# A fused attention and SwiGLU kernel: the last two blocks' down projection by two levels of seven products

## The chip, the cores and the metric

The kernel runs on one core of a Trainium2 chip. Time is device time in microseconds (us), the median of several runs. Engines: TensorE (PE, with its weight loads PEld), VectorE (DVE), ScalarE (ACT), GpSimd (POOL), SyncE (SP, which here only issues DMAs).

## The reference

All in fp32. Attention without softmax, then a feed-forward block on its output, seen as 4608 rows of 512:

```python
kv = np.einsum('bhsd,bhse->bhde', k, v)          # (8, 8, 576, 64) each
out = np.einsum('bhsd,bhde->bhse', q, kv)
rms = np.sqrt(np.mean(out * out, axis=-1, keepdims=True) + 1e-06)
x = (out / rms * g_norm) -> (4608, 512)
g = x @ w_gate                                   # 512 x 1536
silu = g * (1.0 / (1.0 + np.exp(-g)))
return (silu * (x @ w_val)) @ w_out              # 1536 x 512
```

## The kernel before, in words

The 4608 tokens are nine blocks of 512. A block's feed-forward part has an up stage (`x @ w_gate` and `x @ w_val`, silu, product: the hidden values `h`, stored with the hidden dimension on partitions) and a down stage (`h @ w_out`).

A matrix product is not done by eight block products but by seven, in the Winograd form of Strassen's scheme: sums of operand blocks are made first, and the seven products are added up in a chain. The products have the numbers 1 to 7; `CHAIN` (L629) says which of three PSUM tiles (`a`, `b`, `c`) each accumulates in. Class `Quad` (L640) holds one such scheme. `Up` does it for blocks 0 to 2. From block 3 (`PAIRED`) on, two blocks go up together (class `Pair`, L1219), by two levels: `Inner` (L757) does the seven inner products of a group of outer products (`GROUPS`, L765), for both blocks in one matmul of 256 columns; the weights' sums at both levels ("leaves") were made early, written to a scratch tensor `w` in HBM, and are streamed back by `Stream` (L879) into the nine tiles of `t_pool`. `pump` (L895) loads the next as soon as a tile comes free. In the up stage VectorE adds what comes from PSUM, ScalarE copies, and GpSimd makes some further sums: `made1` to `made3` (L837 to L864) add results of the groups, multiply by silu, and make the first-level sums of `h` that the down stage needs.

The down stage (class `Down`, L985) has one level: per block seven products over six hidden pairs with two token halves, 12 matmuls of 128x128 weights (here `h`) by 256 columns (of `w_out` or of its sums `t`, made by GpSimd in `turn_t`). Its rows come out with tokens on partitions and are stored in pieces of up to 512 KB (`Ffn.store`). For the last block (`final`) the last two products and sums are cut in halves, so that the last store is small. Two blocks of a pair go down one after the other (L1439 to L1444).

What sets the order: the whole is traced in Python, and a scheduler places instructions by engine with their semaphores; `in_order` (L135) keeps an engine's instructions as traced, and `tc.issue_after` puts one behind another. For pairs, TensorE's down stage stands as written. SP issues nearly all DMAs, in order; each DMA waits for the one before it on its semaphore, of which there are eight for SP and ACT together. Helpers `add`, `sub` and `mul` have lines 130 to 132, so these sums show under those lines, whoever asks for them.

Of the kernel before, what the change touches and what calls it, by code (L numbers as in the profile page):

```python
# [8 lines left out]
F32 = mybir.dt.float32  # L9
# [9 lines left out]
def kernel(  # L19
# [84 lines left out]
    kvs = [consts.tile([P, NS, D], F32, name=f"kv{i}") for i in range(3)]  # L104
# [29 lines left out]
    @contextmanager  # L134
    def in_order(*engines):  # L135

        traced = nc.cur_bb.bb.instructions
        last = traced[-1]
        yield
        start = next(k for k in reversed(range(len(traced))) if traced[k] is last) + 1  # L140
        before = {}
        for i in traced[start:]:
            if engines and i.engine not in engines:
                continue
            if i.engine in before:
                tc.add_manual_dep(
                    i, before[i.engine].name,
                    mybir.DependencyInfo(mybir.DependencyClass.NoSync, mybir.DependencyReason.DATA), reason="order",
                )
            before[i.engine] = i  # L150

# [488 lines left out]
    class Quad:  # L640


        def __init__(self, steps):
            self.steps = steps
            self.ps, self.room = {}, None

            self.apart = {}

# [3 lines left out]
        def multiply(self, p):  # L652
            name, first = CHAIN[p]
            if first:
                tiles = [PSUMS[name].tile([P, 2, HB], F32, name=name) for _ in range(1 + (name in self.apart))]
                self.ps[name], self.apart[name] = tiles[0], tiles[-1]
            banks = self.ps[name], self.apart[name]
            for e, i in self.order(p):
                lhsT, rhs = self.operands(p, e, i)

                self.ffn.multiplied = nc.tensor.matmul(  # L661
                    banks[e][:, e], lhsT=lhsT, rhs=rhs, start=first and i == 0 and (e == 0 or banks[0] is not banks[1]),
                    stop=i == self.steps - 1, skip_group_check=True,
                )
            getattr(self, f"after{p}", lambda: None)()
# [91 lines left out]
    class Inner:  # L757
# [94 lines left out]
        def made3(self, p, e, q):  # L852
            if p != 4:
                return
            h = h_both[:, :, 2 * self.j : 2 * self.j + 2]
            halves = lambda t: t.rearrange("p (b e) t -> p b e t", b=2)
            c11, c12, c21, c22 = (self.whole(*i) for i in ((1, 1), (3, 1), (3, 0), (1, 0)))

            engine = nc.gpsimd if self.j + 1 < NP else nc.vector
            mul(engine, h[:, :, :, 0:HB], halves(c11), halves(c12))  # L860
            with tc.issue_after(self.ffn.fifth.ins):
                nc.scalar.activation(out=c21, in_=c21, func=ACT.Silu)
            mul(engine, h[:, :, :, HB:BLK], halves(c21), halves(c22))
            self.ffn.ended = self.ffn.a.h_sums(self.j, 1, engine)  # L864

# [13 lines left out]
    class Stream:  # L879
# [15 lines left out]
        def pump(self):  # L895

            while self.next and not self.held[-9]:
                n, j, c = key = self.next.pop(0)
                tile_ = t_tile(key)
                os, ps = JOINT[c]  # L900
                count = len(os) * len(ps)
                self.tiles[key] = tile_.rearrange("p a (b c) -> p (a b) c", c=P)
                self.uses[key] = count
                to = self.tiles[key][:, 0:count].rearrange("p (o i) c -> p o (i c)", o=len(os))
                src = self.dram[:, j, steps_of(OUTERS, os), steps_of(INNERS, ps)].rearrange("p o i c -> p o (i c)")
                nc.sync.dma_start(out=to, in_=src)

        def use(self, n, j, o, p):
            c, i = self.joint[o, p]
            key = n, j, c  # L910
            self.uses[key] -= 1
            if not self.uses[key]:
                self.free(key)
            return self.tiles[key][:, i]
# [4 lines left out]
    stream = Stream()  # L919
# [65 lines left out]
    class Down(Quad):  # L985
        def __init__(self, ffn):
            super().__init__(NP)
            self.ffn = ffn
            self.t = {}
            self.final = ffn.n == NB - 1  # L990
            self.lone = False
            self.opens = None
            self.keeps = False
            if self.final:
                self.apart["c"] = None
# [16 lines left out]
        def multiply(self, p, es=(0, 1)):  # L1012
            if p == 3 and self.lone:
                self.third(es)
                return
# [7 lines left out]
        def third(self, es):  # L1023


            if es[0] == 0:
                tiles = [m_psum.tile([P, 2, HB], F32, name="m") for _ in range(1 + self.final)]
                self.thirds = tiles[0], tiles[-1]
            for e in es:
                for i in range(self.steps):  # L1030
                    lhsT, rhs = self.operands(3, e, i)
                    self.ffn.multiplied = nc.tensor.matmul(  # L1032
                        self.thirds[e][:, e], lhsT=lhsT, rhs=rhs, start=i == 0 and (e == 0 or self.final),
                        stop=i == self.steps - 1, skip_group_check=True,
                    )
            if not self.final:
                add(nc.vector, self.o1[:, :, HD:DM], self.thirds[0], self.u2)
                self.ffn.store(self.o1, 0)
                return
            for e in es:  # L1040
                add(nc.vector, self.o1[:, e, HD:DM], self.thirds[e][:, e], self.u2[:, e])
                self.ffn.store(self.o1[:, e : e + 1, HD:DM], e, slice(HD, DM))

        def after6(self):
            super().after6()
            if self.lone:
                self.add_c(self.u2, self.u2)

        def order(self, p):
            order = [(e, i) for e in range(2) for i in range(self.steps)]  # L1050
            return order if p == 3 and self.final else sorted(order, key=lambda ei: ei[1])
# [17 lines left out]
        def rows(self):  # L1069
            o = ring()  # L1070
            self.o1, self.o2 = o[:, 0:2], o[:, 2:4]

        def after2(self):
            if self.lone:
                self.rows()
            add(nc.vector, self.o1[:, :, 0:HD], self.ps["a"], self.s)
            if self.final:
                self.ffn.store(self.o1[:, :, 0:HD], 0, slice(0, HD))
# [4 lines left out]
        def after7(self):  # L1083
            if not self.lone:
                self.rows()
            u3 = self.piece(2)
            nc.scalar.copy(out=u3, in_=self.ps["b"])
            self.add_c(self.o2[:, :, HD:DM], u3)
# [5 lines left out]
        def after3(self):  # L1094
            self.add_c(self.o1[:, :, HD:DM], self.u2)
            if not self.final:
                self.ffn.store(self.o1, 0)
                return
            for e in range(2):
                self.ffn.store(self.o1[:, e : e + 1, HD:DM], e, slice(HD, DM))  # L1100

        def add_c(self, o, u):

            if not self.final:
                add(nc.vector, o, self.ps["c"], u)
                return
            for e, c in enumerate((self.ps["c"], self.apart["c"])):
                add(nc.vector, o[:, e], c[:, e], u[:, e])

    class Ffn:  # L1110
# [9 lines left out]
        def store(self, o, t, columns=slice(None)):  # L1120
            rows = out[BLK * self.n : BLK * (self.n + 1), columns].rearrange("(t p) d -> p t d", t=T)
# [40 lines left out]
        def down(self, nxt, then={}):  # L1162
# [3 lines left out]
            down.lone = nxt is None  # L1166
            order = (1, 6, 5, 7, 2, 4, 3) if 5 in fill else (1, 5, 6, 7, 2, 4, 3)
            if down.lone:
                order = (1, 5, 6, 2, 7, 3, 4)
            for p in order:  # L1170
# [5 lines left out]
                with tc.issue_after(nxt.multiplied.ins) if self.n == 0 and p in (5, 6) else ExitStack():  # L1176
                    down.multiply(p, *[(0,)] * (p == 3 and down.lone and down.final))
# [14 lines left out]
            if down.lone and down.final:  # L1192
                down.multiply(3, (1,))
# [25 lines left out]
    class Pair:  # L1219


        def __init__(self, n):
            self.n = n
            self.a, self.b = (Ffn(i, blocks[i]) for i in (n, n + 1))
            self.visited = None

        def up(self, fill):

            a = self.a
            a.s1 = s_pool.tile([P, NP, HB], F32, name="s1")  # L1230
# [5 lines left out]
            for i, this in enumerate(units):  # L1236
                for unit, p in this.sequence(last):
                    if unit:
                        visited, self.visited = self.visited, None
                        with tc.issue_after(visited.ins) if visited else ExitStack():  # L1240
                            unit.multiply(p)
                last = this
                fill.get(i + 1, lambda: None)()
            a.down_ = Down(a)
            a.down_.keeps = True
            a.down_.turn_t(5)
# [3 lines left out]
            a.ended = self.ended  # L1250
# [165 lines left out]
    for n in range(PAIRED, NB, 2):  # L1416
# [3 lines left out]
        if after:  # L1420
# [10 lines left out]
            for i in range(8):  # L1431
                fill[12 + i] = lambda i=i, after=after: after[i // 4].load_quarters(i % 4 // 2, (i % 2,))
        pair.up(fill)
        if after:
            after[0].turn()
        if len(after) > 2:
            after[2].load_kv(0)
        with in_order(nc.tensor.engine):
            pair.a.down(after[0] if after else None, {5: pair.second_sums})  # L1439
            if after:  # L1440
                after[1].turn()
            if len(after) > 2:
                after[2].load_kv(1)
            pair.b.down(after[1] if after else None)  # L1444
# [31 lines left out]
```

## Time and profile before

| | us |
|---|---|
| median of three runs (1011.41 to 1013.13) | 1011.48 |
| profiled execution | 1012.7 |
| its span, first to last instruction | 1010.9 |
| TensorE busy in the span | 993.7 |
| VectorE, GpSimd, ScalarE busy | 673.7, 369.6, 232.2 |
| last pair's down stage, TensorE | 934.85 to 1007.37 |

Busy time is the union of an engine's instructions. A row of the profile names line, engine, operation, written and read tile, shape and number; after the bar stand the busy us, the mean ns of one instruction, and the engine's idle time before it with what ended it. An fp32 matmul stands as two records, a transpose as one. The profile reports the granted clock of TensorE as 1.0 throughout.

### The profile page before, as it was taken

The numbers are of one execution on the slowest core, as the hardware profiler recorded it, in microseconds if no ns is written. First come the engines' busy times: TensorE is split into PE (matmuls) and PEld (weight loads), VectorE is DVE, ScalarE is ACT, GpSimd is POOL, SyncE is SP. The second block draws the span as 40 slices with busy tenths as digits, with TensorE's granted clock in tenths as the row PEclk, the third lists the DMA queues.
The fourth block names the chain that finished last, engine by engine and source line by source line (L and its number), as shares of the span: only waits on it lengthen the run. The fifth ranks groups of instructions, "written<-read, shape, count | busy, mean of one in ns | idle before, by whom it ended". The sixth has DMA issues, their size and how long they took to land.

```text
span 1010.9 us, 17078 instructions
## 1 busy us (share of the span) xinstructions
PE 993.7 (98%) x6506; PEld 831.6 (82%) x6506; DVE 673.7 (67%) x1121; ACT 232.2 (23%) x367; POOL 369.6 (37%) x290
## 2 busy tenths in 40 slices
PE   5999999999999999999999999999999999999998
PEld 4544688888888888888888888888888888888887
DVE  2999797589868477656676746666668566666311
ACT  2665111221122311212211121121112121121000
POOL 0000263255544240445456004455660026546600
PEclk9999999999999999999999999999999999999999
DMA  8688653483866855767742464667221654553011
GB/s 220 198 266 260 120 93 136 97 288 97 210 136 122 214 114 158 189 179 182 170 130 42 111 164 135 182 164 191 77 42 43 146 164 144 150 145 101 1 42 42
DMA packets 254290, 143.23 MB, mean 142 GB/s; under 512 B 149504, under 2 KB 236544, under 8 KB 254208
## 3 DMA queue, kind: packets, MB, share of 16 engines
q1 hardware_dynamic: 223488, 138.20, 50.8%
q10 hardware_dynamic: 30656, 3.94, 2.5%
q8 instruction: 52, 0.85, 0.4%
q14 instruction: 30, 0.25, 0.1%
q0 software_dynamic: 64, 0.00, 0.0%
HBM read 104.99 MB, written 28.70 MB: 132 GB/s over the span
## 4 chain that ended last, share of the span: by engine, by line
PE 75%; DMA 1%; POOL 0%; SPq 0%; issue 0%; DVE 0%; POOLq 0%
PE b L816 22%; PE b L661 20%; PE c L816 11%; PE c L661 9%; PE a L816 5%; PE a L661 5%; PE m L431 1%; PE m L1032 1%; PE m L370 1%; DMA ld<-in_v_dram 1%; POOL t L131 0%; SPq L312 0%; PE b L370 0%; PE b L431 0%; PE a L431 0%
## 5 line engine op out<-in xcount | busy, mean ns | idle before, releaser
L816 PE MATMUL b<-arena,t 128*128 128x256 f32 x1008 | 244.5, 381 | 0.0
L816 PEld LDWEIGHTS b<-arena,t 128*128 128x128 f32 x1008 | 190.1, 190 | 29.6 <-DVE r L130 2.4
L130 POOL TENSOR_TENSOR r<-r 128x256 f32<-128x256 f32 (+1 forms) x90 | 94.7, 1054 | 246.1 <-DVE r L130 154.9
L130 DVE TENSOR_TENSOR r<-b,r 128x512 f32<-128x512 f32 (+1 forms) x234 | 138.9, 606 | 60.1 <-PE b L816 54.8
L130 DVE TENSOR_TENSOR r<-c,r 128x512 f32<-128x512 f32 (+1 forms) x170 | 104.5, 623 | 81.9 <-PE c L816 40.1
L132 POOL TENSOR_TENSOR arena<-r 128x1024 f32<-128x1024 f32 (+1 forms) x54 | 102.1, 1904 | 112.3 <-DVE r L130 67.9
L131 POOL TENSOR_TENSOR t<-wo 128x512 f32<-128x512 f32 x54 | 76.9, 1445 | 167.8 <-DVE wo L130 105.9
L130 DVE TENSOR_TENSOR r<-a,r 128x512 f32<-128x512 f32 x93 | 59.2, 636 | 108.3 <-PE a L661 70.7
L816 PE MATMUL c<-arena,t 128*128 128x256 f32 x504 | 122.5, 379 | 0.0
L131 DVE TENSOR_TENSOR arena<-arena 128x512 f32<-128x512 f32 (+3 forms) x96 | 104.3, 1101 | 20.0 <-PE b L661 17.7
L816 PEld LDWEIGHTS c<-arena,t 128*128 128x128 f32 x504 | 95.6, 190 | 13.5 <-issue 0.3
L661 PE MATMUL b<-wo,arena 128*128 128x256 f32 x432 | 98.1, 382 | 0.2
L661 PE MATMUL b<-t,arena 128*128 128x256 f32 x432 | 96.2, 379 | 0.0
L661 PEld LDWEIGHTS b<-wo,arena 128*128 128x128 f32 x432 | 81.2, 190 | 12.5 <-DVE arena L132 0.9
L661 PEld LDWEIGHTS b<-t,arena 128*128 128x128 f32 x432 | 82.1, 190 | 11.2
L830 ACT COPY r<-b 128x512 f32<-128x512 f32 x54 | 31.7, 586 | 189.9 <-PE b L816 189.9
L131 POOL TENSOR_TENSOR t<-arena 128x512 f32<-128x512 f32 x36 | 51.1, 1432 | 56.2 <-PE c L661 21.9
L816 PE MATMUL a<-arena,t 128*128 128x256 f32 x252 | 66.1, 379 | 0.0
L816 PEld LDWEIGHTS a<-arena,t 128*128 128x128 f32 x252 | 47.9, 190 | 6.5
L661 PE MATMUL c<-t,s 128*128 128x256 f32 x216 | 48.1, 379 | 0.0
L661 PE MATMUL a<-wo,arena 128*128 128x256 f32 x216 | 48.1, 379 | 0.0
L661 PEld LDWEIGHTS a<-wo,arena 128*128 128x128 f32 x216 | 41.0, 190 | 5.6
(115 smaller groups left out, 1242.9 us busy)
## 6 DMA issues: line engine op xcount, KB each, us to landing
t<-w SPq DMA_DIRECT2D x180, 256.0 KB, 3.1
out_dram<-r SPq DMA_DIRECT2D x17, 512.0 KB, 2.9
ld<-in_k_dram SPq DMA_DIRECT2D x26, 288.0 KB, 4.6
ld<-in_v_dram SPq DMA_DIRECT2D x26, 288.0 KB, 6.1
t<-w SPq DMA_DIRECT2D x54, 128.0 KB, 2.3
ld<-in_moe_w_gate_dram SPq DMA_DIRECT2D x12, 512.0 KB, 4.6
ld<-in_moe_w_val_dram SPq DMA_DIRECT2D x12, 512.0 KB, 4.7
ld<-in_moe_w_out_dram SPq DMA_DIRECT2D x12, 512.0 KB, 4.8
```

The costliest lines, as they stand in the source:

```text
L130: add = lambda e, o, a, b: e.tensor_tensor(out=o, in0=a, in1=b, op=OP.add)
L131: sub = lambda e, o, a, b: e.tensor_tensor(out=o, in0=a, in1=b, op=OP.subtract)
L132: mul = lambda e, o, a, b: e.tensor_tensor(out=o, in0=a, in1=b, op=OP.mult)
L370: self.positions = nc.tensor.matmul(self.kv_ps[r][u * D : (u + 1) * D, g, :], lhsT=k[:, u, c, :], rhs=v[:, u, c, :], start=(c == 0), stop= ...
L431: self.multiplied = nc.tensor.matmul(self.ps[i][u][p : p + D, t, j, :], lhsT=self.qt[rows, tile_t, head, p : p + D], rhs=kvs[b % 3][rows, ...
L661: self.ffn.multiplied = nc.tensor.matmul(banks[e][:, e], lhsT=lhsT, rhs=rhs, start=first and i == 0 and (e == 0 or banks[0] is not banks[1 ...
L816: self.ffn.multiplied = nc.tensor.matmul(ps[:, i], lhsT=stream.use(self.ffn.n, self.j, o, p), rhs=self.operand(o, p), start=first and i == ...
L830: copied = nc.scalar.copy(out=dst, in_=ps)
L1032: self.ffn.multiplied = nc.tensor.matmul(self.thirds[e][:, e], lhsT=lhsT, rhs=rhs, start=i == 0 and (e == 0 or self.final), stop=i == self ...
```

## The change

Only the last two blocks (7 and 8) are treated differently; they go up as before. `Down` loses its special forms for the last block.

- Both blocks go down together, by two levels of seven products (`Last`, a kind of `Inner`, and `Deep`). Now the weights are the stationary operand and `h` of both blocks moves, 2 x 128 columns; results come out with the output dimension on partitions, in four groups of outer products (1, 2), (6, 5), (7), (4, 3).
- The second-level sums of `w_out` are made by GpSimd in the up stage of the pair, one side step after certain products (`tick`): the first-level sum in place, twelve sums kept in SBUF (`kept`), and for the outer products 5, 7 and 4 nine "turned blocks" of sums, which go to a scratch tensor `leaf` in HBM by SP (two stores, six products after their sums) and come back through the stream as 21 tiles.
- First-level sums of `h` are made in place by GpSimd 12 products after the values; second-level sums of `h` by VectorE in the down stage (`sum_x`, `outer`), which also does the last unit's (`second`, `turn`).
- In the end two quarters of the result are turned by VectorE in 32x32 blocks and stored by 16 DMAs each on ACT's and SP's queues (`send`); the other two by 16 PE transposes, copied by ScalarE and VectorE and stored by eight DMAs of SP (`turn_back`).
- The three `kv` tiles become one (a turned block's sums borrow one of them).

```diff
-    kvs = [consts.tile([P, NS, D], F32, name=f"kv{i}") for i in range(3)]
+    kv_room = consts.tile([P, 3, NS * D], F32, name="kv")
+    kvs = [kv_room[:, i].rearrange("p (j d) -> p j d", d=D) for i in range(3)]
...
+            if self.ffn.deep:
+                self.ffn.deep.made(self.j, engine, c21, halves(c21), halves(c22), h)
+                return
...
+    class Last(Inner):
+        GROUPS = ((1, 2), (6, 5), (7,), (4, 3))
...
+            for c in cs:
+                for i, o in enumerate(self.outers):
+                    self.ffn.multiplied = nc.tensor.matmul(
+                        ps[:, i], lhsT=self.deep.weight(o, p, c), rhs=self.deep.operand(o, p, c),
+                        start=first and c == 0 and i == 0, stop=c == 2, skip_group_check=True,
+                    )
+            stream.pump()
...
+            if p in self.ADDED:
+                add(nc.vector, dst, ps, dst)
+            elif self.g == 3:
+                add(nc.vector, dst, ps, self.shared[2][:, :, :, e, q])
+            elif self.g == 0:
+                nc.scalar.copy(out=dst, in_=ps)
+            else:
+                add(nc.vector, dst[:, 0], ps[:, 0], self.onto[:, :, e, q])
+                if n > 1:
+                    nc.scalar.copy(out=dst[:, 1], in_=ps[:, 1])
...
+        def turned_block(self, i, c):
...
+            def send():
+                with behind(nc.sync.engine):
+                    nc.sync.dma_start(out=to[:, 0:5], in_=t)
+                    nc.sync.dma_start(out=to[:, 5:7], in_=more)
+
+            def differences():
+                sub(nc.gpsimd, t[:, 4], t[:, 0], t[:, 1])
+                sub(nc.gpsimd, more, t[:, 2:4], t[:, 1:2].to_broadcast([P, 2, P]))
+                self.sends.append((self.count + 6, send))
...
+        FIRST = {0: (0, 1, 3), 1: (0, 2, 4), 2: (1, 4), 3: (0, 2, 4, 5)}
+        TURNS = {0: (0, 1), 1: (), 2: (4,), 3: (0, 2, 4, 5)}
+
+        def tick(self):
+            g, e = divmod(self.count % 28, 7)
+            self.count += 1
+            if self.sends and self.sends[0][0] <= self.count:
+                self.sends.pop(0)[1]()
+            due = self.due and self.due[0][0] <= self.count
+            if due and (g, e) in ((2, 5), (2, 6)):
+                step = self.due.pop(0)[1]
+            elif e in (self.TURNS if self.count > 28 else self.FIRST)[g]:
+                step = self.due.pop(0)[1] if due else self.later.pop(0) if self.later else None
...
+        def made(self, j, engine, c21, g, v, h):
...
+            steps = [lambda: add(engine, a21, a21, a22), lambda: sub(engine, a21, a21, a11)]
...
+            self.due += [(self.count + 12, step) for step in steps]
...
+        def send(self, room, half, cols, queue):
...
+                    for r in range(4):
+                        dst = out[row : row + HB, col + 32 * r : col + 32 * (r + 1)]
+                        queue.dma_start(
+                            out=dst.rearrange("(c i) j -> i c j", i=32), in_=t[32 * r : 32 * (r + 1), f, e]
+                        )
+
+        def turn_back(self, e, q, final=False):
+            ps = m_psum.tile([P, 2, 2, P], F32, name="m")
+            for o in range(2):
+                for f in range(2):
+                    nc.tensor.transpose(ps[:, o, f], self.shared[3][:, o, f, e, q], ident)
+            to = self.rows[:, e, q]
+            if final:
+                for o in range(2):
+                    nc.vector.tensor_copy(out=to[:, o], in_=ps[:, o])
+            else:
+                nc.scalar.copy(out=to, in_=ps)
...
+                nc.sync.dma_start(out=blocks_[row : row + P, :, col : col + P], in_=to[:, o])
+
+        def down(self):
...
+            run(self.turn(2, 0))
+            m(0, 1, (0, 1))
+            m(0, 2, (0, 1))
+            m(0, 1, (2,))
+            self.sum_x(0, 1, 2)
+            m(0, 2, (2,))
+            m(0, 6)
+            self.sum_x(1, 1, 2)
+            m(0, 5)
+            self.sum_x(2, 1, 2)
+            self.second()
+            run(self.turn(2, 1))
+            m(0, 7)
+            self.outer(5, ((0, 0), (0, 1)))
+            m(0, 3)
+            m(1, 1)
+            self.sum_x(0, 6, 5)
...
+            m(2, 4)
+            nc.vector.transpose(out=room[:, 0], in_=c11)
+            self.send(room[:, 0], 0, 0, nc.scalar)
+            m(3, 6)
+            add(nc.vector, c22, u3, c22)
+            m(3, 5)
+            nc.vector.transpose(out=room[:, 1], in_=c22)
+            self.send(room[:, 1], 1, 1, nc.sync)
+            m(3, 2)
+            m(3, 7)
+            self.rows = ring().rearrange("p (e q) (o f d) -> p e q o f d", e=2, o=2, f=2)
+            m(3, 3)
+            self.turn_back(0, 0)
+            self.turn_back(1, 1)
+            m(3, 4)
+            self.turn_back(1, 0)
+            self.turn_back(0, 1, True)
...
+        if pair.deep:
+            stream.leaves(pair.deep)
+            pair.up(fill)
+            with in_order(nc.tensor.engine, nc.vector.engine):
+                pair.deep.down()
+            continue
```

## The prediction

> **What bounds the kernel now.** I read first the page's busy shares and its chain that ended last, then the chain in order of time for the last 80 us, then the groups of instructions and the timeline there. The whole page:
>
> ```profile
> span 1010.9 us, 17078 instructions
> PE 993.7 (98%) x6506; PEld 831.6 (82%) x6506; DVE 673.7 (67%) x1121; ACT 232.2 (23%) x367; POOL 369.6 (37%) x290
> ```
>
> TensorE is the bound; the other engines have room on average. The chain at the end (start, length, engine, tile, line, matmul records), and the timeline behind it:
>
> ```profile
> 992.00 5.18 PE b L661 x24
> 997.18 2.59 PE m L1032 x12
> 999.77 5.18 PE b L661 x24
> 1004.95 2.60 PE m L1032 x12
> 1007.58 0.42 DVE L130 TENSOR_TENSOR r<-m,r 128x256 f32<-128x256 f32 x1 [7.35 <-PE m L1032]
> ```
>
> One fp32 product of 12 matmuls is 24 records and 5.18 us: 0.216 us a record, 0.432 a matmul. The last two blocks' down stage is 14 such products, starts at 934.85 and issues its last at 1007.37: 72.5 us with no gap. After it stand an eviction (0.42, done at 1008.00) and a store; the span ends 2.88 later. What this stage leaves to the others:
>
> ```profile
> 930.00:951.00 21.00, 21.00 (x98) 18.25 (x97) 9.73 (x13) 2.05 (x3) 14.04 (x10) 1.00 0.00 1
> 951.00:972.00 21.00, 21.00 (x99) 18.47 (x99) 4.43 (x5) 1.35 (x3) 4.61 (x4) 1.00 0.07 26
> 972.00:990.00 18.00, 18.00 (x85) 15.86 (x84) 2.51 (x3) 1.17 (x2) 0.00 (x0) 1.00 0.08 29
> ```
>
> Columns are length, then busy us of PE, PEld, DVE, ACT and POOL: VectorE and GpSimd are nearly idle where the change puts work. Prices, by shape:
>
> ```profile
> L494 PE MATMUL m<-ident,r 128*128 128x128 f32 x16 | 2.3, 274 | 0.3 <-DVE r L132 0.3
> L131 DVE TENSOR_TENSOR arena<-arena 128x896 f32<-128x896 f32 x3 | 3.3, 1089 | 0.1
> L132 DVE TENSOR_TENSOR arena<-r 128x1024 f32<-128x1024 f32 x2 | 2.4, 1222 | 0.1
> L130 DVE TENSOR_TENSOR s<-arena 128x256 f32<-128x256 f32 x1 | 0.4, 424 | 0.0
> L386 DVE STREAM_TRANSPOSE r<-ld 128x1024 f32<-128x1024 f32 x16 | 19.3, 1226 | 0.0
> L132 POOL TENSOR_TENSOR arena<-r 128x1024 f32<-128x1024 f32 x10 | 23.4, 2363 | 19.0 <-DVE r L130 19.0
> L131 POOL TENSOR_TENSOR t<-wo 128x512 f32<-128x512 f32 x4 | 5.1, 1274 | 4.5 <-DVE arena L131 4.5
> L130 POOL TENSOR_TENSOR r<-r 128x256 f32<-128x256 f32 x24 | 17.4, 727 | 71.0 <-DVE r L130 70.4
> ```
>
> A PE transpose has one record: 2.3/16 = 0.144 us. VectorE from SBUF: 0.42 at 256 elements, 1.09 at 896, so 0.96 at 768 and 0.69 at 512; an eviction is 0.69 (512) or 0.41 (256). GpSimd: 0.73 at 256, 1.27 at 512, so 1.00 at 384 and 0.46 at 128.
>
> **What the Trainium skill says.** "SBUF — State Buffer", Who interferes with whom: a VectorE instruction with two SBUF inputs and a GpSimd instruction that reads SBUF exclude each other for the whole instruction; one with at most one SBUF input doesn't. The trace agrees: at 356.59 a 1536-element difference took 2.42 beside GpSimd's sums instead of 1.75, while no eviction from PSUM in the last pair's up stage is longer than 0.69 beside GpSimd. "DMA: Bandwidth & Descriptors", Specifications: below 512 B a transfer costs a read-modify-write; no run here shows 128-byte writes to HBM. No page bears on the order of the products.
>
> **The change, part by part.** By the built order nothing before the last pair is moved, nor are its waits; all that follows is after 800 us.
>
> *TensorE.* 168 matmuls go, 147 of the same size come (49 products, 3 steps each): -21 x 0.432 = -9.07 us. 16 transposes come; 8 stand between the last two products, +1.15. The last matmul would issue at 934.87 + 63.46 + 1.15 = 999.5.
>
> *GpSimd, up stage.* From 803 on its list goes from 65 sums (34 of 256, 15 of 512, 16 of 1024: 82 us, the last at 955) to 103 (9 of 128, 33 of 256, 12 of 384, 33 of 512, 16 of 1024: 120 us, nearly all of it by 938). I walked its queue in the built order, unit by unit (21.15 us each): 17.5, 18.2, 19.3, 21.2, 19.3 us busy, before 11.4. In the fourth unit it is full, and the made-over sums behind a side sum start up to 2.6 us late, but their readers come some 5 us later: 0 us, as long as its rows hold. The six differences in place in the output weight start at 803.5, beside the last three 896-element sums of VectorE, and by the lock those end near 811 rather than 807.4; the product that reads the third of them keeps 0.4 us, the next waits of evictions 0.2 to 1.0: 0 us, at most 1.
>
> *DMA.* 18 stores and 21 loads of leaves (192 KB or less) go on SP's queue. Each load has its tile 10 us or more before its product (landings here: 2.8 us): 0.
>
> *VectorE, down stage.* 33 sums of 768 (31.6), 6 of 512 (4.2), 5 of 1024 (6.1), 13 evictions of 512 (9.0), 11 of 256 (4.6), two transposes (2.4), two copies (0.8): 58.7 us in a stage of 66, in a fixed order; before, 20. It is late once. From the last eviction of the up stage at 935.07 to the first quarter of outer 5 stand 0.69 + 1.22 + 2 x 0.69 + 2 x 0.96 + 0.69 + 4 x 0.96 + 1.22 + 4 x 0.69 + 0.69 + 0.96 = 15.4 us; the lock with GpSimd's last two sums adds about 1.1: 951.5. TensorE has then issued 37 of its matmuls, 934.87 + 37 x 0.432 = 950.8, so it waits 0.7. Later sums come 1.5 to 6 us ahead of their products.
>
> *The end.* Last matmul issued at 999.5 + 0.7 + 0.1 (restart) = 1000.3. Then as before 0.2, an eviction (0.69), four transposes with their semaphore (0.16 + 0.58), 0.2, two copies (0.41 + 0.33): 1002.9, and the last store. Before, 3.5 us lay between last matmul and end; now 0.2 + 0.69 + 0.74 + 0.2 + 0.74 + 2.9 = 5.5, that is +2.0. The span would end at 1005.8.
>
> *Stores in turned pieces.* The two quarters that VectorE transposes go out in 32 DMAs of 32 KB in 128-byte pieces, 16 on ACT from 986.8, 16 on SP from 990.9, and SP's last eight stores queue behind. Bounds: issue takes 0.49 each where SP alone loads quarters of q (eight in 3.92), about 0.85 where ACT and SP issue together:
>
> ```profile
> 473.40 3.92 SPq L333 DMA_DIRECT2D ld<-in_q_dram  x8
> 786.11 7.34 ACTq L522 DMA_DIRECT2D arena<-r  x8
> arena<-r SPq DMA_DIRECT2D x72, 64.0 KB, 3.5
> ld<-in_q_dram SPq DMA_DIRECT2D x32, 32.0 KB, 2.3
> ```
>
> Landing lies between 2.3 (same size, reads) and 3.5 (twice the size). At 0.55 and 2.7 SP is through its sends near 1000, and the last store goes 0.3 late. At 3.5 each, four sends in a chain on one semaphore (eight are shared by both queues) end at 990.9 + 14 = 1004.9: 2 us lost. I take 0.3: **span 1006.1**, 4.8 less than 1010.9. The profiled execution took 1012.7, 1.8 above its span; the median of the three runs, 1011.48, is 0.6 above it. I take the difference to the median: **1006.8 us**, range of this case 1005.4 to 1008.3.
>
> **Rivals.**
> 1. *The 128-byte stores set the end.* Place: SP's queue behind its sends. The last store should go at 1002.9; it is late when a send takes over 0.58 to issue (990.9 + 16x + 7 x 0.39) or over 3.0 to land (990.9 + 4L), 4 us for each us of landing. It eats the gain at L = 4.2 or x = 0.88, and is slower than before by over 0.2% only from L = 4.8 or so: 1013.5 to 1016. For it: the read-modify-write that the skill names; against it: SP has the queue alone after some five sends, where 0.49 was seen, and at most four of its DMAs are then in flight. In between it gives 1008 to 1011.
> 2. *GpSimd becomes the bound of the up stage.* It has no spare time in the fourth unit. If every row were 10% longer, the walk through the queues gives +3.7 us (1010.5), at 15% +8 (1015). Against: its rows scatter by under 2% where VectorE reads PSUM, and only the 128 and 384 sizes are interpolated.
> 3. *VectorE is late in the down stage.* 58.7 us of 66 leave little: 5% longer sums cost 0.7 us, 10% 2.6 (1009.4), 20% 7 (1013.8). Against: 512 and 896 elements in other strides lie on one line.
> 4. *The products don't shrink.* The built order shows 147 matmuls and 16 transposes, so this is out.
>
> **How the numbers follow.** Main case 0.64; stores late, 1008 to 1011: 0.14, and beyond 1013.5: 0.04; GpSimd or VectorE 8% or more over: 0.13, of it 0.05 over 1013.5; better than 1005.4 (no wait, no late store): 0.05. A measurement of this kernel tells about 0.2%, 2 us, from no change. Faster than 1009.5: main, better, half of the late stores and a third of the engines: 0.79. Within: 0.12. Slower: 0.09. The range leaves out some 2 in 10 at both ends: 1005.3 to 1010.8.
>
> **What would show it.** 147 matmuls from 934.9, a single wait of TensorE near 951 of under 2 us, last product near 1000.3; GpSimd 18 to 21 us busy in each unit of 21.15, and no wait of TensorE there; VectorE without idle time from 936 to 987; the last stores near 1003. It is wrong if TensorE shows waits in the up stage, if the down stage has waits of over 2 us in sum, or if SP's last stores are issued after 1004.

## The result and the profile after

The changed kernel takes 1006.28 us (median of four runs, 1005.85 to 1006.68) against 1011.57 of the kernel before in the runs beside it: ratio 0.9939, 95% interval 0.9924 to 0.9954, so 5.3 us faster; 4.7 to 4.8 was forecast. Its profiled execution took 1006.5 us. The page's first lines:

```profile
span 1004.2 us, 17235 instructions
PE 987.2 (98%) x6480; PEld 825.1 (82%) x6480; DVE 715.3 (71%) x1174; ACT 233.3 (23%) x370; POOL 408.3 (41%) x328
```

The span is 6.7 shorter, but 1.5 of that stands in the trace before the last pair's up stage, where the change puts nothing but GpSimd's first sums (from 802.04 on) and TensorE has no wait: that stage starts at 807.59 before and at 806.12 after. In the fourteen profiles of this study that start lies between 806.1 and 809.6. From it on the traces agree closely (the up stage takes 127.26 us before, after and in all runs but two), so below each run, whose trace is one execution, is also given as **start of the last pair's up stage to the end of the span**: 203.29 before, 198.05 after, that is -5.24, as the medians have it.

This difference is all in the down stage and behind it. The chain of waits of the changed kernel, in order of time (start, length, engine, tile, line, records):

```profile
948.75 0.88 DVE arena L131
...
949.67 7.61 PE b L894 x34
...
994.83 0.87 PE m L1101 x8
995.71 2.61 PE b L894 x12
998.34 0.70 DVE r L131
...
999.17 0.64 PE m L1101 x4
999.84 0.42 DVE r L1105
1000.26 0.33 DVEq L1765
```

The stage's first product starts at 933.37. At 949.67 TensorE waits once, for VectorE's first quarter of outer 5 (0.35 us lost, the restart included); eight transposes take 0.87; the last matmul is issued by 998.13. The stage takes 64.76 us instead of 72.52. From there to the end are 6.04 us, before 3.51: -7.76 + 2.53 = -5.23.

What the stages leave to the engines (length, then busy us of PE, PEld, DVE, ACT, POOL; clock; DMA): the fullest stretch of the up stage, then the down stage:

```profile
874.00:895.00 21.00, 21.00 (x99) 18.47 (x99) 14.02 (x25) 4.31 (x7) 20.42 (x19) 1.00 0.57 178
...
933.50:950.00 16.50, 16.42 (x77) 13.97 (x76) 15.96 (x19) 2.82 (x4) 3.40 (x3) 1.00 0.09 25
950.00:971.00 21.00, 21.00 (x99) 18.49 (x98) 19.81 (x27) 1.70 (x4) 0.00 (x0) 1.00 0.23 65
971.00:988.00 17.00, 17.00 (x81) 14.96 (x80) 15.87 (x23) 0.38 (x1) 0.00 (x0) 1.00 0.27 69
```

GpSimd is all but full near 880 (20.42 of 21), and in the down stage VectorE, which had little to do there before, is busy for 51.6 of the first 54.5 us. Two engines stand close behind TensorE.

The end as SP's queue sees it (start, length from first to last issue, queue, line, count), and the landing time of SP's sends:

```profile
984.83 7.96 ACTq L1092 DMA_DIRECT2D out_dram<-r  x16
988.97 7.85 SPq L1092 DMA_DIRECT2D out_dram<-r  x16
996.91 4.60 SPq L1111 DMA_DIRECT2D out_dram<-r  x8
```

```profile
out_dram<-r SPq DMA_DIRECT2D x16, 32.0 KB, 1.7
```

The sends go 0.50 us apart on both queues, also while both issue, and land in 1.7 us on either. From SP's first send to the end of the span are 15.2 us, and for 12.5 of them its 24 DMAs are issued one behind another with only two gaps (0.48 and 0.34).

### The profile page after: what moved, and what is told of

Same layout as the page of the kernel before. It is cut to its first block, busy times and chain, and to the rows that moved or that the text cites. A ratio compares the mean times of both kernels' runs of the same rounds, so it can differ in the third digit from the quotient of the medians.

```text
span 1004.2 us, 17235 instructions
## 1 busy us (share of the span) xinstructions
PE 987.2 (98%) x6480; PEld 825.1 (82%) x6480; DVE 715.3 (71%) x1174; ACT 233.3 (23%) x370; POOL 408.3 (41%) x328
## 4 chain that ended last, share of the span: by engine, by line
PE 74%; DVE 2%; DMA 1%; issue 0%; DVEq 0%; SPq 0%
PE b L818 22%; PE b L663 16%; PE c L818 11%; PE c L663 8%; PE a L818 5%; PE a L663 4%; PE b L894 3%; PE c L894 1%; PE m L436 1%; PE m L375 1%; PE a L894 1%; DMA ld<-in_v_dram 1%; DVE arena L131 1%; DVE arena L132 0%; DMA t<-w 0%; DVE arena L133 0%
## 5 line engine op out<-in xcount | busy, mean ns | idle before, releaser
L818 PE MATMUL b<-arena,t 128*128 128x256 f32 x1008 | 244.6, 381 | 0.3 <-DMA t<-w 0.3
L131 DVE TENSOR_TENSOR r<-b,r 128x512 f32<-128x512 f32 (+1 forms) x247 | 146.1, 603 | 66.7 <-PE b L818 55.3
L132 POOL TENSOR_TENSOR t<-wo 128x512 f32<-128x512 f32 x45 | 64.1, 1447 | 162.4 <-DVE wo L131 103.8
L132 DVE TENSOR_TENSOR arena<-arena 128x512 f32<-128x512 f32 (+4 forms) x117 | 122.4, 1064 | 9.3 <-PE b L663 6.9
L663 PE MATMUL b<-wo,arena 128*128 128x256 f32 x336 | 76.8, 382 | 0.2
L663 PE MATMUL b<-t,arena 128*128 128x256 f32 x336 | 74.8, 379 | 0.0
L663 PEld LDWEIGHTS b<-wo,arena 128*128 128x128 f32 x336 | 62.9, 190 | 10.0 <-DVE arena L133 0.9
L663 PEld LDWEIGHTS b<-t,arena 128*128 128x128 f32 x336 | 63.8, 190 | 8.7
L663 PE MATMUL b<-arena 128*128 128x256 f32 x192 | 45.5, 380 | 0.0
L663 PE MATMUL b<-arena,t 128*128 128x256 f32 x192 | 45.4, 379 | 0.0
L1485 PE MATMUL b<-arena 128*128 128x512 f32 (+1 forms) x104 | 43.5, 561 | 0.6 <-ACT arena L500 0.6
```

The costliest lines, as they stand in the source:

```text
L131: add = lambda e, o, a, b: e.tensor_tensor(out=o, in0=a, in1=b, op=OP.add)
L132: sub = lambda e, o, a, b: e.tensor_tensor(out=o, in0=a, in1=b, op=OP.subtract)
L663: self.ffn.multiplied = nc.tensor.matmul(ps[:, e], lhsT=lhsT, rhs=rhs, start=first and i == 0 and e == 0, stop=i == self.steps - 1, skip_g ...
L818: self.ffn.multiplied = nc.tensor.matmul(ps[:, i], lhsT=stream.use(self.ffn.n, self.j, o, p), rhs=self.operand(o, p), start=first and i == ...
L1485: nc.tensor.matmul(t, lhsT=w[f // 2][:, i, P * (f % 2) : P * (f % 2 + 1)], rhs=x[:, i, of], start=(i == 0), stop=(i == NS - 1),)
```

## The experiments

All are edits of the changed kernel. "Against the changed kernel" is the difference of up-stage start to end in the trace.

| run | median us | ratio to before (95%) | up stage to end | against the changed kernel | expected |
|---|---|---|---|---|---|
| the changed kernel | 1006.28 | 0.9939 (0.9924 to 0.9954) | 198.05 | | |
| 21 matmuls more | 1015.68 | 1.0030 (1.0018 to 1.0042) | 206.75 | +8.70 | +8.3 to +8.7 |
| two steps of three | 1005.48 | 0.9933 (0.9918 to 0.9948) | 195.40 | -2.65 | -3.9 |
| no sums | 1006.30 | 0.9943 (0.9928 to 0.9957) | 197.71 | -0.34 | -0.4 to -0.7 |
| both of these | 991.00 | 0.9788 (0.9771 to 0.9805) | 181.13 | -16.92 | -18.4 |
| outer sums twice | 1016.66 | 1.0047 (1.0030 to 1.0064) | 208.54 | +10.49 | +9.7 |
| kept sums twice | 1011.99 | 0.9995 (0.9986 to 1.0004) | 203.14 | +5.09 | +4.4 |
| kept sums three times | 1022.95 | 1.0106 (1.0091 to 1.0121) | 213.63 | +15.58 | +15.1 |
| side sums one place earlier | 1007.31 | 0.9946 (0.9927 to 0.9965) | 197.52 | -0.53 | -0.3 to -0.7 |
| turned blocks stored at once | 1014.63 | 1.0026 (1.0016 to 1.0035) | 204.16 | +6.11 | +2.8 |
| sends on one queue | 1011.13 | 0.9990 (0.9983 to 0.9997) | 201.44 | +3.39 | +2.5 |
| no sends | 1006.95 | 0.9945 (0.9930 to 0.9960) | 197.78 | -0.27 | 0 |
| not turned back | 1007.40 | 0.9950 (0.9935 to 0.9965) | 198.31 | +0.26 | -1.4 |

Differences under 2 us can't be told by the medians; there the trace decides, and only on what it shows of the waits.

### What the matmuls are worth

```diff
-            for c in cs:
+            for c in [c for c in cs for _ in range(2 if c == 1 and p in (1, 6, 5) else 1)]:
```

> One step of three of the seven inner products is done twice (21 matmuls more, the number that the change took away; these products' values change). Theory (TensorE sets the stage, VectorE is just behind): each of the 21 is paid in full, 21 x 0.432 = 9.07 us, less the wait near 950, which goes: +8.3 to +8.7 us against the changed kernel: about 1014.8 us. Rival (VectorE's order of sums sets most of the stage): +3 us or less, 1009.

Measured +8.70. The wait near 950 is gone (TensorE needs the quarter later), so 21 matmuls cost 8.70 + 0.35 = 9.05 us, 0.431 each: the price that the forecast gave to the 21 taken away. The rival, with 3 us or less, is out. In the other direction:

```diff
+                    lhsT, rhs = self.deep.weight(o, p, c), self.deep.operand(o, p, c)
+                    if c == 1:
+                        continue
```

> The middle of the three steps of each product of the last down stage is left out: 49 matmuls of 147, 49 x 0.432 = 21.2 us of TensorE's work (the products are then sums over two thirds of the hidden dimension). Theory (TensorE sets the stage, but VectorE with 58.7 us of work stands close behind it): only about 4 us are won before VectorE's order of sums becomes the bound, and TensorE then waits some 15 us in all: about 1002.4 us. Rival (TensorE alone counts, VectorE has room): -21 us, 985. Rival (something other than TensorE set the stage already): 1006.

21.2 us of matmuls go and the trace is 2.65 shorter: one eighth. TensorE's waits in this run (engine, tile and line, for whom; us in total, times, longest; L897 is the matmul's line here):

```profile
PE b L897 <- DVE r L131: 5.5, 4, 2.5
PE b L897 <- DVE arena L131: 3.5, 1, 3.5
PE m L1104 <- ACT r L1110: 2.0, 1, 2.0
```

The time goes into waits for VectorE's sums and evictions, and at the end for a copy by ScalarE. What VectorE itself has to do shows from the stage's first product to the end of its second transpose, which SP's sends wait for (columns as above, VectorE's busy time third; the changed kernel, then this run):

```profile
933.37:988.94 55.57, 55.49 (x257) 48.38 (x256) 52.58 (x67) 4.89 (x9) 3.53 (x3) 1.00 0.20 54
936.10:988.99 52.89, 43.43 (x181) 34.21 (x180) 51.76 (x68) 4.89 (x9) 3.52 (x3) 0.97 0.20 55
```

VectorE is idle for 2.99 us of that stretch in the changed kernel and for 1.13 in this run: its own 51.8 us are left, and the stretch is 2.68 shorter. SP's first send goes at 989.02, and the span ends 15.2 us behind it, as in the changed kernel, so these 2.68 us are the gain. The 3.9 that was expected would have needed VectorE with no idle time at all.

Behind the longest wait TensorE is slow for a while (the wait is 3.67 us between the starts of two records, with the restart; 3.5 of it stand in the profile as idle time):

```profile
952.40:956.80 4.40, 4.40 (x13) 3.62 (x14) 3.94 (x6) 0.37 (x1) 0.00 (x0) 0.63 0.15 45
953.60:956.90 3.30, 3.30 (x9) 2.67 (x8) 2.83 (x5) 0.37 (x1) 0.00 (x0) 0.50 0.21 60
```

The granted clock is 0.50 in the second stretch, and eight matmul records stand 0.43 apart instead of 0.216: 1.7 us of TensorE's time. VectorE, for which TensorE waits again later, stands idle for 0.47 us at 953.80 and otherwise goes on, so little of the missing gain is due to the slow spell. Is it VectorE's sums, or another limit behind the matmuls (evictions, PSUM tiles, leaves)? Leaving out only the sums, and then both:

```diff
-            for o in os:
+            for o in ():
...
-            for k, q in parts:
+            for k, q in ():
```

> VectorE's 33 sums of h of 768 elements in the down stage are left out (31.6 us of its work; the products then take other values of h). Theory (TensorE's count of products sets the stage, VectorE is late once by 0.35 us): the single wait near 950 goes and nothing else: -0.4 to -0.7 us against the changed kernel, 1005.6 to 1005.9. Rival (VectorE's sums pace the down stage): several us less, 1003 or lower.

> The middle step of each product of the last down stage (49 matmuls, 21.2 us) and VectorE's 33 sums of h there are both left out. Theory (two engines in balance: leaving out the matmuls alone won about 3 us because VectorE then set the pace): now nearly the whole 21 us come, the walk through the queues gives -18.4 against the changed kernel, the last 2 to 3 us going to SP's issues at the end: about 988 us. Rival (what kept the stage long without the matmuls was not VectorE's sums but evictions, PSUM tiles, loads or ScalarE): 1000 us or more.

The sums alone are worth 0.34, the wait near 950, which is gone. The matmuls alone are worth 2.65, both together 16.92: while one engine's work stays, leaving out the other's gives little. What remains of the 21 us in the run without both stands at the end. SP's queue:

```profile
974.31 7.85 SPq L1095 DMA_DIRECT2D out_dram<-r  x16
982.26 4.27 SPq L1114 DMA_DIRECT2D out_dram<-r  x8
```

Its 24 DMAs follow each other with a single gap (0.34), and again the span ends 15.2 us behind the first. TensorE's last matmul starts only 5.1 us behind that send, in the changed kernel 9.0. The chain of waits goes through ScalarE's sends from 970.86 on, and then:

```profile
978.45 1.60 DMA out_dram<-r
980.06 0.58 ACT r L1110
```

ScalarE issues its 16 sends in order and only then makes the copy that frees the PSUM tile for the last transposes. Either queue would hold the end here; no run separates them. In the changed kernel ScalarE's sends end at 992.79 and this costs nothing.

### How much room VectorE and GpSimd have

```diff
-            for k, q in parts:
+            for k, q in parts + parts:
```

> The 12 sums of h for the single outer products (768 elements, 0.96 us each) are made twice on VectorE in the down stage: 11.5 us more work there (a difference made in place is then taken twice, so its value changes). Theory (VectorE just keeps ahead, with 1.5 to 6 us in hand): the room is used up and TensorE waits several times: the walk through the queues gives +9.7 us against the changed kernel, about 1016. Rival (VectorE has some 8 us of room in the stage, as its 58.7 of 66 us of busy time say): +3 to +4 us, 1010. Rival (sums hidden throughout): 1006.3.

Measured +10.49 for 11.5 us of added sums. TensorE's waits for VectorE, then the stretch of VectorE's work as above, then SP's last eight stores (ns to issue one, shortest, median and longest):

```profile
PE b L894 <- DVE r L131: 4.8, 3, 3.0
PE b L894 <- DVE arena L131: 1.8, 1, 1.8
```

```profile
936.89:1001.72 64.83, 58.22 (x257) 49.23 (x256) 62.63 (x79) 4.89 (x9) 3.51 (x3) 0.97 0.17 46
```

```profile
L1111 SPq DMA_DIRECT2D out_dram<-r x8: 372/410/1677, 1009.7 to 1013.9; - x8
```

With the restarts the waits cost TensorE 1.97, 3.20, 1.27 and 0.82 us near 955, 977, 987 and 994, and behind the longest (3.20) eight records are again 0.43 apart; VectorE goes on working meanwhile. Its stretch is 9.26 us longer, for 10.05 us more of busy time (neighbouring instructions overlap a little): less than 1 us of the added work found room, although 2.99 us were idle in the changed kernel. In this edit a group's quarters are made once more only after its last, so a product waits for the whole second pass. The other 1.25 us of the 10.49 are behind the stage: the last store takes 1.68 us to issue instead of 0.43.

```diff
-                        lambda o=o, b=b, x=x, k=k, n=n: sub(
+                        lambda o=o, b=b, x=x, k=k, n=n: [sub(
...
-                        )
+                        ) for _ in range(2)]
```

> Each of the 12 kept sums of GpSimd (384 elements, 1.00 us) in the last pair's up stage is made twice, with the same values: 12 us more work for GpSimd, none for the others. Theory (GpSimd's sums cost nothing only because they fit into the units of 21.15 us, with little room left): walking the queues in the built order with the rows' durations, the sums at the end of the list run past the up stage and TensorE waits for them near 942 to 954, +4.4 us against the changed kernel: about 1010.6 us. Rival (GpSimd has room enough, nothing waits for it): 1006.3 us. Rival (GpSimd is already the bound of the up stage): +12 us, 1018.

> The same 12 sums three times: 24 us more for GpSimd. Theory: beyond the room every further us is paid; the walk through the queues gives +15.1 us against the changed kernel, with the first waits of TensorE near 887: about 1021 us, and a difference of some 10.7 to the run with each sum twice (12 us of work added). Rival (room enough): 1006 to 1008. Rival (GpSimd the bound from the start): +24 us, 1030.

+5.09 for the first 12 us and +10.49 for the next. Of the first, 1.3 is again the last store:

```profile
L1111 SPq DMA_DIRECT2D out_dram<-r x8: 372/410/1723, 1001.8 to 1006.0; - x8
```

So 3.8 of the first 12 us are paid, some 8 were free, and of the next 12 nearly every us is paid: 11.8, of which 1.7 is TensorE's half pace behind a wait of 4.11 us, where VectorE in turn stands idle for 2.74 us instead of 1.05. How GpSimd's work is paid is the instructive part. With each sum twice the up stage still takes 127.26 us; the sums run over into the down stage and meet VectorE there (VectorE's and GpSimd's timelines; a row can hold several instructions, the length is from the first to the last):

```profile
937.31 2.65 DVE L131 TENSOR_TENSOR arena<-arena 128x512 f32<-128x512 f32 x1
```

```profile
939.38 6.19 POOL L132 TENSOR_TENSOR ld<-wo 128x384 f32<-128x384 f32 x4
```

VectorE's sums of 512 elements that take 0.69 alone take 2.65 and 1.37, and TensorE then waits for VectorE in three places (0.70, 1.13 and 1.91 us). Only with three times the sums does the up stage itself grow, by 5.9.

### The wait near 950

```diff
-        FIRST = {0: (0, 1, 3), 1: (0, 2, 4), 2: (1, 4), 3: (0, 2, 4, 5)}
+        FIRST = {0: (0, 1, 3), 1: (0, 2, 4), 2: (1, 3, 5), 3: (0, 2, 4, 5)}
```

> GpSimd's side sums get three places instead of two in one stretch of the first unit, so that its list ends one place sooner and the last two kept sums no longer run beside VectorE's first sums of the down stage; the same sums are made. Theory (the 0.35 us wait of TensorE near 950 comes from VectorE's first sums, which the lock with those two sums lengthens by some 1.0 us): VectorE's product at the start of the stage takes 1.23 us instead of 1.62 and its next sum 0.69 instead of 1.30, and the wait is gone: -0.3 to -0.7 us against the changed kernel, 1005.6 to 1006.0. Rival (these lengths have another cause, or the wait is for something else): the wait stays, 1006.3.

VectorE's timeline at the start of the down stage, and below it GpSimd's last sums, of the changed kernel and then of this run:

```profile
934.42 1.62 DVE L133 TENSOR_TENSOR arena<-r 128x1024 f32<-128x1024 f32 x1
936.15 1.30 DVE L131 TENSOR_TENSOR arena<-arena 128x512 f32<-128x512 f32 x1
933.93 2.96 POOL L132 TENSOR_TENSOR ld<-wo 128x384 f32<-128x384 f32 x2
```

```profile
935.80 1.62 DVE L133 TENSOR_TENSOR arena<-r 128x1024 f32<-128x1024 f32 x1
937.52 0.69 DVE L131 TENSOR_TENSOR arena<-arena 128x512 f32<-128x512 f32 x1
935.33 1.00 POOL L132 TENSOR_TENSOR ld<-wo 128x384 f32<-128x384 f32 x1
```

One of GpSimd's two late sums moved out of the way, not both (it makes one at 935.33), and just one of the two long instructions became short: 0.6 us, enough for the wait near 950 to go. That is the lock of "SBUF — State Buffer" in the Trainium skill (section Who interferes with whom) switched off for one instruction. By the trace this version is 0.53 us better than the changed kernel; in the medians that can't be told.

### The stores of the turned blocks

```diff
-                self.sends.append((self.count + 6, send))
+                send()
```

> The stores of the turned blocks are put right behind their sums in the order of SP's queue instead of six products later; nothing else is altered. Theory (SP's queue is in order, so a store that waits for GpSimd's sums holds the loads of leaves behind it, and TensorE then waits for a leaf): the walk through the queues gives two waits of 1.4 us near 880 and 924, +2.8 us against the changed kernel: about 1009.0 us. Rival (the loads have 10 us in hand and absorb it): 1006.3 us.

+6.11, twice what was expected and enough to be slower than before (1.0026, from 1.0016 up). The chain of waits goes through loads of leaves in three places:

```profile
857.98 4.22 DMA t<-w
...
882.06 3.96 DMA t<-w
...
927.20 3.99 DMA t<-w
```

SP's queue near the second, in this run and in the changed kernel (line 947 is a store of a turned block, 1236 the loads of leaves):

```profile
856.94 13.01 SPq L1236 DMA_DIRECT2D t<-w  x14
879.45 0.33 SPq L947 DMA_DIRECT2D leaf<-s  x1
```

```profile
876.39 0.32 SPq L947 DMA_DIRECT2D leaf<-s  x1
877.49 13.95 SPq L1236 DMA_DIRECT2D t<-w  x11
```

The store waits at the head of the queue for GpSimd's sums, and no load goes from 870 to 880.5; in the changed kernel they go on from 877.5. The loads on the chain then take 4.0 to 4.2 us to land, against 3.1 and 3.2 as the medians for 192 and 256 KB in the changed kernel. TensorE loses 0.65, 2.5 and 2.4 us in the three places. The expectation had the hold-up, but two places with 1.4 us each; the prediction had the loads land in 2.8 us, which would explain it, but whether the forecast rests on that is open.

### The end

```diff
-            self.send(room[:, 0], 0, 0, nc.scalar)
+            self.send(room[:, 0], 0, 0, nc.sync)
```

> All 32 stores of 32 KB in pieces of 128 bytes go on SP's queue instead of 16 on ACT's and 16 on SP's. Theory (each takes 0.50 us of the queue's time to issue, which hides only while SP is through before the last rows are ready near 1000.6): SP has 32 x 0.5 = 16 us of issue from about 988 and the last eight stores of 0.5 us each stand behind it, so the end comes 2 to 3 us later: about 1008.8 us. Rival (the issue pace is shared between the two queues, so one queue alone issues faster, or the landing and not the issue sets the end): 1006.3 us.

```profile
987.56 15.85 SPq L1092 DMA_DIRECT2D out_dram<-r  x32
```

One queue has the same pace, 32 sends in 15.85, and all eight last stores come behind them, 0.52 us apart: the last goes out 19.6 us behind the first send, in the changed kernel 16.2 (984.83 to 1001.08). That is the +3.39. The expectation named 0.5 us for sends and last stores alike, and this gives 16 + 3.5 and so 3.3; why the forecast was only 2.5 is open.

```diff
-            for f in range(2):
+            for f in range(0):
```

> The 32 stores of 32 KB in pieces of 128 bytes are left out (two quarters of the last blocks' result are not written). Theory (landing of 1.7 us and issue of 0.50 us keep them off the path): 1006.3 us, within 0.5. Rival (they cost the end something on SP's queue or in HBM): 1 to 2 us less, 1004.5 to 1005.5.

```diff
-            ps = m_psum.tile([P, 2, 2, P], F32, name="m")
-            for o in range(2):
-                for f in range(2):
-                    nc.tensor.transpose(ps[:, o, f], self.shared[3][:, o, f, e, q], ident)
-            to = self.rows[:, e, q]
...
+            to = self.shared[3][:, :, :, e, q]
```

> The 16 transposes by TensorE at the end and the copies behind them are left out: the last quarters are stored as they come out of the sums (their output is then not turned). Theory (the end costs 2.56 us more than before: 8 transposes between the last two products, and 4 transposes and two copies behind the last): -1.15 for the eight, -1.22 for the chain behind the last eviction, but four stores instead of two then stand behind it on SP's queue, +1.0: -1.4 us against the changed kernel, 1004.9 us. Rival (the stores alone set the end): 1006.3. Rival (SP's issues don't matter): -2.4, 1003.9.

Without the sends the end comes 0.27 earlier; without the transposes and copies 0.26 later. In the second run SP's queue is the reason (its last eight stores; line 1102 here; then the ns to issue one, shortest, median and longest):

```profile
998.34 4.84 SPq L1102 DMA_DIRECT2D out_dram<-r  x8
L1102 SPq DMA_DIRECT2D out_dram<-r x8: 372/423/1038, 998.3 to 1002.1; - x8
```

24 DMAs stand behind each other from 990.40 to 1003.18, with a single gap (0.35), and the span ends 2.7 later. So the rival that the stores alone set the end was right for this run. The last store starts 0.38 us earlier than in the changed kernel, counted from the start of the up stage, but takes 1.04 us to issue instead of 0.43, and that is why the end is later. In the changed kernel SP's queue alone would thus end some 0.4 us earlier, and the chain of eviction, transposes and copies alone some 0.3: shortening one of the two gives next to nothing.

Last stores that take 1.0 to 1.7 us to issue stand in three runs (this one, outer sums twice, kept sums twice). In all three the two stores before them take 2.8 to 3.5 us to land, in the changed kernel 2.1; why is open.

## Why the prediction was right

The terms held, each within 0.5 us; the closeness of the median (1006.28 for 1006.8) is in part luck. The span was forecast at 1006.1 and is 1004.2, of which 1.5 lie before the up stage; and the step from the span to the median was taken as 0.6, where 2.1 was measured.

- **TensorE, -9.07**: held; 0.431 a matmul when 21 are added. The eight transposes took 0.87 (0.109 each), not 1.15: the price, 0.144, was a row's busy time by its number, and a row's busy time has the latency of each group's last one in it.
- **The wait near 951**: right place, right engine, right cause, 0.35 instead of 0.8 with the restart. The lock's 1.1 us was measured as 0.39 + 0.61 = 1.0; the sums in front were a little shorter than forecast.
- **The lock at the start of the up stage, 0**: held. The three differences of 896 elements took 6.31 us beside GpSimd's sums instead of 3.33 and ended at 808.92, which is 810.4 in the time of the kernel before (forecast: near 811), and TensorE did not wait. Before and after:

```profile
804.09 3.33 DVE L131 TENSOR_TENSOR arena<-arena 128x896 f32<-128x896 f32 x3
802.61 6.31 DVE L132 TENSOR_TENSOR arena<-arena 128x896 f32<-128x896 f32 x3
```

- **GpSimd, up stage, 0**: held. The units were forecast at 17.5, 18.2, 19.3, 21.2 and 19.3 us busy; stretches of 21 us (the last of 22) show 15.9, 17.7, 18.8, 20.4 and 19.4, and TensorE has no wait there.
- **VectorE, down stage**: late once, as forecast; but not without idle time from 936 to 987, since 2.9 us are left over.
- **The end, +2.3 with the late stores**: measured 2.53. The 0.3 for the sends is about what the run without them shows (0.27), but by other sizes: they land in 1.7 instead of 2.7 and take 0.50 to issue instead of 0.55, while the stores behind them take 0.5 each instead of 0.39. That the two agree is luck as well: at 0.55 and 2.7 neither bound of the forecast's first rival (0.58 to issue, 3.0 to land) makes the last store late, so its 0.3 was an allowance.
- **The sum**: -9.07 + 1.15 + 0.8 + 2.0 + 0.3 = -4.8 was forecast; -9.07 + 0.87 + 0.35 + 2.53, and 0.1 of small gaps, is -5.2. Two terms came out smaller and one larger, which takes off part of the error.
- **DMA of leaves, 0**: held with the stores six products late. The run with stores at once shows what that place is worth, 6.1 us, more than the whole gain.
- **Rival 1** fell: leaving the 128-byte pieces out gains 0.27 us. "DMA: Bandwidth & Descriptors" in the Trainium skill (section Specifications) has a read-modify-write below 512 B; 32 KB in such pieces landed here in 1.7 us, where reads of the same size took 2.1. No run stores the same 32 KB in larger pieces, so a small price isn't excluded. **Rivals 2 and 3** were the right ones to fear: of 10 us of work added to VectorE less than 1 found room, of 12 us added to GpSimd about 8.

## What to carry to other kernels

Taking work from the bounding engine pays in full only as far as the next engine lets it: here 21 matmuls fewer were worth 9 us, and 49 more away only 2.65, because the sums that replace products had filled VectorE, and the stores at the end start behind VectorE's last results. Before such a trade, add up the second engine's work in that stage alone, in its fixed order, and test both engines by leaving out each one's work and then both. Where DMAs share a queue in order, a store that waits for its data belongs behind the loads that others wait for.

## What was not expected of the hardware

- Behind some long waits TensorE falls to half pace. Behind waits of 2.28, 3.20, 3.67 and 4.11 us (in four places of three runs) about eight matmul records stood 0.43 apart instead of 0.216, at once or after up to five records at full pace, with a granted clock of 0.50 in stretches of 3.3 us there; behind waits of 0.6 to 2.2 us, and one of 2.64, none did. "TensorE: Matmul & The Clock Gate" in the Trainium skill (Part 1, What's actually happening) states half clock after an idle window of about 3.4 us that runs freely; the trace agrees in kind, but 2.28 us was enough once. Such a spell costs TensorE 1.7 us. In three of the four places VectorE went on working meanwhile and TensorE soon waited for it again, so hardly any of this reached the end; in the fourth, VectorE stood idle as well.
- Writes to HBM in 128-byte pieces were quick here: 1.7 us for 32 KB, beside 2.0 for the last stores of 128 KB.
- GpSimd's work beyond its stage cost TensorE time through VectorE, not directly: with each kept sum made twice, two of VectorE's sums of 512 elements took 2.65 and 1.37 us instead of 0.69.
